# A spectral branch's first product as seven half-size products, beside an attention loop, on one Trainium2 core

## The chip, the core and the metric

The kernel runs on one core of one Trainium2 chip. The engines are named as in the profile: PE (TensorE, matrix products), DVE (VectorE), ACT (ScalarE), POOL (GpSimd) and SP (SyncE, which here issues every transfer); 16 DMA engines move data between device memory and the on-chip memory. The metric is the device time of one execution in microseconds.

## The reference

Two branches share nothing but the output, whose halves they fill. Branch A is attention with 32 heads of 32 and one key and value head (S = 2048, D = 1024); branch B is a two-dimensional Fourier mixing, written as matrix products.

```python
q = (x @ wq).reshape(B, S, H, Dh).transpose(0, 2, 1, 3)
k, v = x @ wk, x @ wv
p = softmax(einsum("bhqd,bkd->bhqk", q, k) * Dh ** -0.5)
a_out = einsum("bhqk,bkd->bhqd", p, v).transpose(0, 2, 1, 3).reshape(B, S, H * Dh) @ wo
...
a = einsum("bsd,ed->bse", xB, dft_hid_re)      # first product, real part
b = einsum("bsd,ed->bse", xB, dft_hid_im)      # first product, imaginary part
y = einsum("ts,bse->bte", dft_seq_re, a) - einsum("ts,bse->bte", dft_seq_im, b)   # second product
out = concatenate([a_out, y], axis=-1)
```

## The kernel before, in words

**Two kinds of work.** The attention loop runs over 32 units (a block of 512 queries and a group of four heads) of 32 steps each. A step `n` makes the scores of 128 queries against 1024 keys (`scores`, two matmuls into `pss`), takes the negated row maximum of them on DVE (`nm`), sums the exponentials of rows on ACT (`row_sums`, in place in `pss`, which has two buffers), and makes transposed scores of an earlier unit (`expo`, two matmuls into `pst`, which has one buffer, then an exponential on ACT into `p`). Every eighth step ends with `pv`, 16 products of probabilities with values, which DVE adds into `ov`.

Everything else is *filler*: the key, value and query projections, both products of branch B and the output projection. It is a list of groups (`add`, line 226). A group of 24 matmuls fills one 128 x 512 tile `psb` in PSUM: eight chunks of 128 rows, each with three matmuls, because each float32 factor is split in a high and a low part (`rh`, `rl` for the right factor of 128 x 512; `mh`, `ml` for the left one, of which one item covers four chunks). `take(n)` issues the next n filler matmuls; after a group's last one its `post` empties the tile.

**What sets the order.** Instructions of an engine run in program order (`Ordered`, line 42), and the order is written out by the loop at line 685. `level` (line 681) spreads the filler evenly: what is left after the prologue is divided over the 1024 steps, seven shares in each eight steps, none at the step with `pv`. `aside` (line 316) lets a group run on when a bank is wanted near its start or its end. Two PSUM banks (`ps_b`) serve the filler, `pv` and a small transpose in turn (`bank`, line 268).

**How factors come.** Two lines of items, `RL` for right and `ML` for left factors (lines 220 and 221), each with four steps: load from device memory, add a second source on GpSimd where there is one (`comb`; `nothing` for `RL`), cast to the high part (`hi`), subtract to get the low part (`lo`). Each step is issued a fixed number of filler matmuls ahead of the item's due time: 40, 40, 14 and 8 for `RL`, 52, 36, 27 and 21 for `ML`. Casts are on ACT before the loop and on DVE in it (line 153), subtractions on DVE. An item with `save` has both parts stored, and a later item with `pre` fetches them ready made. `load_y` (line 212) brings a tile that a group's `post` adds to, up to four at a time (`NY`).

**The stage that is changed.** `stage1` (line 383) makes the first product. Its four column blocks (r, e), real or imaginary part and half of the columns, each take 16 row blocks of one group of 24. `post` evicts the tile on ACT with the sign of r, stores it, and on GpSimd adds it to, or subtracts it from, an earlier block: these sums (`NAMES`, line 378) are the right factors of the second product. `stage2` (line 435) makes that product in seven products of half size in each direction (the table `PRODUCTS`, line 31: left terms, right terms, outputs with signs), each in two halves of the summed dimension that are joined in `h`; its left factors are added on GpSimd. Positions in the filler: key, value and query projections 0 to 864, `stage1` 864 to 2400, `stage2` to 5088, output projection to 5664, the last block's to 5856. The prologue ends at position 494.

Of the kernel before, what the change touches and what calls it, by code (L numbers as in the profile page):

```python
# [29 lines left out]

PRODUCTS = [
# [21 lines left out]
class Item:  # L53


    def __init__(self, srcs, save=None, pre=None):
        self.srcs, self.save, self.pre = srcs, save, pre
        self.need = self.last = self.due = self.t = None


class Group:


    def __init__(self, left, right, post, rows=P, ys=()):
        self.left, self.right, self.post, self.rows, self.ys = left, right, post, rows, ys


@with_exitstack
def tile_kernel(ctx: ExitStack, tc, xT, wq, wkv, wo, xbT, wT, cT, out):
# [19 lines left out]
    xb_d = [[[dram.tile([P, 4, P], F32, name=f"xb_{s}_{q}_{a}") for a in range(2)] for q in range(2)] for s in range(NC)]  # L89
# [14 lines left out]
    NR0, NM0, NY = 3, 3, 4  # L104
# [112 lines left out]
    def nothing(it):  # L217
        pass

    RL = Line(NR0, NR, (40, 40, 14, 8), load_r, nothing, hi_r, lo)  # L220
# [5 lines left out]
    def add(gs):  # L226

        for g in gs:
            i0 = len(groups) * 24
# [3 lines left out]
            for c, it in enumerate(g.right):  # L233
                if it.need is None:
                    it.need = i0 + 3 * c
                    p0 = prev["set"]
                    it.due = min(it.need, p0 + (i0 - p0) * (c + 1) // 8)
# [12 lines left out]
    prev = {"set": -200, "this": 0}  # L250

# [13 lines left out]
    cur = {"at": 0, "bank": None}  # L265
# [20 lines left out]
    def product(g, ps, j):  # L286
# [3 lines left out]
        te.matmul(ps[:g.rows], a, r.lo if w == 1 else r.hi, start=j == 0, stop=j == 23)  # L290

    def take(n):
        for _ in range(n):
            i, j = divmod(pos["fill"], 24)
            if i >= len(groups):
                return
            g = groups[i]
# [8 lines left out]
            if j == 23:  # L306
# [20 lines left out]
    qp = pool(ctx, "qp", 1)  # L327
# [4 lines left out]
    def kv_post(b):  # L332
        cols = slice(b * W, (b + 1) * W)

        def post(ps):
            kv = qp.tile([2 * DH, W], F32, name="kv")
            act.activation(kv, ps[:2 * DH], AF.Copy)
            dve.tensor_copy(kst[0:DH, cols], kv[0:DH])
            kl = qp.tile([DH, W], F32R, name="kl")
# [38 lines left out]
    NAMES = {}  # L378
    for _, nt, _ in PRODUCTS:
        key = tuple(nt)  # L380
        NAMES[key] = [dram.tile([P, W], F32, name=f"r{len(NAMES)}_{s}") for s in range(NC)]

    def stage1():
        seen = []
        for r, e in ((0, 0), (1, 1), (0, 1), (1, 0)):
            ws = [Item([(lambda c=c, r=r, e=e: wT[r, e, c], 1)]) for c in range(ND)]
            sg = -1 if r else 1
            todo = [k for k in NAMES if len(k) == 2 and all(t[:2] in seen + [(r, e)] for t in k)
                    and any(t[:2] == (r, e) for t in k)]
            seen.append((r, e))  # L390
# [376 lines left out]
```

## Time and profile before

| | |
|---|---|
| median of three runs (lowest to highest) | 2896.22 us (2896.21 to 2896.61) |
| the profiled execution: its time, its span | 2893.22 us, 2891.4 us |
| granted TensorE clock, mean of the span | 0.999 |
| ACT busy, share of the span | 2279.2 us, 79% |
| DVE busy, share of the span | 1995.0 us, 69% |
| transfers in the span | 485.03 MB, mean 168 GB/s |
| transfers issued in `stage1` by line of the page | loads 32 + 32, saves 64, fetches 192, results 64, sums 80 read and 80 written |

The page gives, in this order: busy time of each engine, the span in 40 slices, the DMA queues, the chain of work that ended last, the costliest groups of instructions, and the transfers. A row of the groups reads: source line, engine, operation, the tile that is written `<-` the tiles that are read, shapes, `x` the number of instructions, then busy time in us and the mean of one in ns, then the idle time of the engine just before them and what ended it. All engine instructions pass through the helper at line 50, so rows are told apart by their tiles, and a group's window in time by the counts of its rows. A row of the timeline has the start, the duration, the instruction and in brackets the idle time before it. A row of the waits has the waiting engine and tile, the releaser, the total in us, how often, and the longest. Matmuls overlap in PE's pipeline, so that their pitch, the distance between starts, is shorter than the duration shown. SPq is SP's queue.

### The profile page before, as it was taken

The numbers are of one execution on the slowest core, as the hardware profiler recorded it, in microseconds if no ns is written. First come the engines' busy times: TensorE is split into PE (matmuls) and PEld (weight loads), VectorE is DVE, ScalarE is ACT, GpSimd is POOL, SyncE is SP. The second block draws the span as 40 slices with busy tenths as digits, with TensorE's granted clock in tenths as the row PEclk, the third lists the DMA queues.
The fourth block names the chain that finished last, engine by engine and source line by source line (L and its number), as shares of the span: only waits on it lengthen the run. The fifth ranks groups of instructions, "written<-read, shape, count | busy, mean of one in ns | idle before, by whom it ended". The sixth has DMA issues, their size and how long they took to land.

```text
span 2891.4 us, 39967 instructions
## 1 busy us (share of the span) xinstructions
PE 2839.5 (98%) x14096; PEld 1957.6 (68%) x14096; DVE 1995.0 (69%) x2593; ACT 2279.2 (79%) x3342; POOL 467.8 (16%) x342
## 2 busy tenths in 40 slices
PE   7999999999999999999999999999999999999999
PEld 5876667666666766666666666766666666666666
DVE  6866677555565656888788887778887787765510
ACT  4688888888888888888887887878878788888851
POOL 0000000011121223222223230022232220120000
PEclk9999999999999999999999999999999999999999
DMA  8865455555666667455355453264454432454455
GB/s 301 284 197 168 168 183 184 166 169 186 200 206 218 226 221 238 122 153 164 107 173 160 131 176 114 86 191 140 138 149 139 146 122 84 142 168 130 134 155 169
DMA packets 318025, 485.03 MB, mean 168 GB/s; under 512 B 33664, under 2 KB 98688, under 8 KB 317824
## 3 DMA queue, kind: packets, MB, share of 16 engines
q1 hardware_dynamic: 317824, 482.48, 53.3%
q8 instruction: 111, 1.82, 0.3%
q14 instruction: 90, 0.74, 0.1%
HBM read 351.54 MB, written 129.76 MB: 166 GB/s over the span
## 4 chain that ended last, share of the span: by engine, by line
PE 45%; issue 6%; DVE 4%; ACT 3%; DMA 3%; POOL 2%; SPq 0%; POOLq 0%; ACTq 0%
PE psb L50 29%; PE pst L50 9%; PE pss L50 8%; DVE nm L50 2%; DMA y<-y 1%; ACT p L50 1%; POOL y L50 1%; ACT pss L50 1%; DVE mh L50 1%; DMA m<-in_cT_dram 1%; SPq L50 0%; DVE ml L50 0%; DMA y<-r 0%; DVE rl L50 0%; POOL m L50 0%
## 5 line engine op out<-in xcount | busy, mean ns | idle before, releaser
L50 DVE TENSOR_REDUCE nm<-pss 128x1 f32<-128x1024 f32 x1024 | 1250.6, 1222 | 361.9 <-PE pss L50 358.8
L50 ACT ACTIVATE p<-pst 128x1024 f32<-128x1024 f32 x1024 | 1054.0, 1029 | 395.8 <-PE pst L50 389.3
L50 ACT ACTIVATE pss<-pss,nm 128x1024 f32<-128x1024 f32 x1024 | 1117.5, 1091 | 104.5 <-DVE nm L50 95.2
L50 PE MATMUL psb<-rh,mh 128*128 128x512 f32 (+1 forms) x1916 | 754.9, 394 | 10.3 <-ACT rh L50 8.0
L50 PE MATMUL psb<-rh,ml 128*128 128x512 f32 (+1 forms) x1916 | 754.4, 394 | 0.5 <-DVE ml L50 0.5
L50 PE MATMUL psb<-rl,mh 128*128 128x512 f32 (+1 forms) x1916 | 754.0, 394 | 0.3 <-DVE rl L50 0.3
L50 PE MATMUL pst<-qst,kst 128*128 128x512 f32 x2048 | 660.8, 403 | 17.3 <-ACT p L50 16.7
L50 PE MATMUL pss<-kst,qst 128*128 128x512 f32 x2048 | 657.5, 402 | 12.4 <-ACT pss L50 11.7
L50 PEld LDWEIGHTS pss<-kst,qst 128*128 128x128 f32 x2048 | 372.7, 188 | 202.6 <-issue 86.4
L50 PEld LDWEIGHTS pst<-qst,kst 128*128 128x128 f32 x2048 | 367.3, 188 | 155.3 <-ACT p L50 77.9
L50 PE MATMUL psb<-p,v 128*32 128x512 f32 x4096 | 466.0, 595 | 0.0
L50 PEld LDWEIGHTS psb<-rh,mh 128*128 128x128 f32 (+1 forms) x1916 | 358.8, 187 | 97.5 <-ACT rh L50 9.0
L50 PEld LDWEIGHTS psb<-rl,mh 128*128 128x128 f32 (+1 forms) x1916 | 358.8, 187 | 87.0 <-DVE rl L50 1.4
L50 PEld LDWEIGHTS psb<-rh,ml 128*128 128x128 f32 (+1 forms) x1916 | 358.7, 187 | 86.8 <-DVE ml L50 1.4
L50 PEld LDWEIGHTS psb<-p,v 128*32 128x32 f32 x4096 | 120.0, 109 | 276.0 <-issue 269.1
L50 POOL TENSOR_TENSOR m<-m,m 128x512 f32<-128x512 f32 x160 | 215.3, 1352 | 462.5 <-DMA m<-in_cT_dram 398.4
L50 DVE TENSOR_TENSOR ov<-ov,psb 128x512 f32<-128x512 f32 x96 | 66.0, 688 | 292.9 <-PE psb L50 292.9
L50 ACT ACTIVATION_READ_ACCUMULATOR pss<-pss,nm 128x1 f32 x1024 | 213.5, 209 | 0.0
L50 DVE TENSOR_TENSOR ml<-m,mh 128x512 fp32r<-128x512 f32 (+1 forms) x274 | 198.1, 723 | 4.0 <-ACT mh L50 3.6
L50 POOL TENSOR_TENSOR y<-y,h 128x512 f32<-128x512 f32 x64 | 91.7, 1443 | 564.8 <-DVE h L50 505.9
L50 DVE CAST mh<-m 128x512 fp32r<-128x512 f32 x267 | 145.2, 544 | 21.6 <-POOL m L50 15.1
L50 POOL MEMSET qst<- 32x2048 f32 x32 | 58.5, 1833 | 564.7 <-PE pst L50 454.6
(63 smaller groups left out, 798.2 us busy)
## 6 DMA issues: line engine op xcount, KB each, us to landing
m<-in_cT_dram SPq DMA_DIRECT2D x384, 256.0 KB, 3.7
r<-r SPq DMA_DIRECT2D x112, 256.0 KB, 3.7
mh<-xb SPq DMA_DIRECT2D x96, 256.0 KB, 3.9
ml<-xb SPq DMA_DIRECT2D x96, 256.0 KB, 4.1
y<-y SPq DMA_DIRECT2D x96, 256.0 KB, 2.9
y<-r SPq DMA_DIRECT2D x80, 256.0 KB, 3.1
r<-y SPq DMA_DIRECT2D x80, 256.0 KB, 2.0
qst<-qh SPq DMA_DIRECT2D x64, 256.0 KB, 5.7
```

The costliest lines, as they stand in the source:

```text
L50: return lambda *a, **k: self.tc.keep_in_program_order(f(*a, **k))
```

## The change

The first product is made for two pairs of column blocks, `((0, 0), (1, 1))` and then `((1, 0), (0, 1))`. For each pair, seven products of half the size in rows, in the summed dimension and in columns take the place of eight (table `STAGE1`: name, left terms, right terms, and for each output the partial sum that it adds to, the sign, and where it goes). A product has eight groups, one for each row block of a half, and a group has four chunks, so 12 matmuls. The tables' counts over the seven products are 12 left terms, 12 right terms and 8 outputs, of which 7 add to a partial sum.

Partial sums (`t`, `u2`, `u3`, `u4`) are stored in device memory and loaded again; DVE adds the PSUM tile to the loaded one, only the first product's tile is evicted on ACT. Left and right factors with two or three terms are added on GpSimd in `comb`, now for `RL` too; the third source of a left item and the second and third of a right one lie in tiles `h`, which `stage2` uses later. The combined left and right factors of `p6` are also stored as they are (`raw`), because `p3` and `p4` use them. The first pair saves its split left factors, the second fetches them. `NY` becomes 6. The real and imaginary blocks keep their sign, so `PRODUCTS` has other signs and another order, and `stage2` needs no copies with a changed sign. A group's length is now its own (`g.n`), which also enters `add`, `take` and `aside`. The tiles of the key and value eviction come from the pool `yp`, and their own pool is gone.

```diff
 PRODUCTS = [
-    ([(1, 1, 1)], [(1, 0, 1), (0, 0, -1)], [(0, 0, 1), (1, 0, 1)]),
...
-    ([(1, 0, 1), (1, 1, -1)], [(1, 0, 1), (1, 1, 1)], [(0, 0, 1)]),
+    ([(0, 0, 1), (1, 1, 1)], ((0, 0), (1, 1)), [(0, 0, 1), (1, 1, 1)]),
+    ([(0, 1, 1), (1, 1, 1)], ((0, 0),), [(1, 0, 1), (1, 1, -1)]),
...
+    ([(1, 1, 1)], ((1, 0), (0, 0)), [(0, 0, -1), (1, 0, -1)]),
+]
+SUB = ((0, 0), (1, 1))
...
+STAGE1 = [
+    ("p1", [(0, 0, 1)], [(0, 0, 1)], [(None, 1, "t")]),
+    ("p2", [(0, 1, 1)], [(0, 1, 1)], [("t", 1, (0, 0))]),
+    ("p6", [(1, 0, 1), (1, 1, 1), (0, 0, -1)], [(1, 1, 1), (1, 0, -1), (0, 0, 1)], [("t", 1, "u2")]),
+    ("p7", [(0, 0, 1), (1, 0, -1)], [(1, 1, 1), (1, 0, -1)], [("u2", 1, "u3")]),
+    ("p5", [(1, 0, 1), (1, 1, 1)], [(1, 0, 1), (0, 0, -1)], [("u2", 1, "u4"), ("u3", 1, (1, 1))]),
+    ("p3", [(0, 1, 1), ("p6", -1)], [(1, 1, 1)], [("u4", 1, (0, 1))]),
+    ("p4", [(1, 1, 1)], [("p6", 1), (0, 1, -1)], [("u3", -1, (1, 0))]),
 ]
...
-    xb_d = [[[dram.tile([P, 4, P], F32, name=f"xb_{s}_{q}_{a}") for a in range(2)] for q in range(2)] for s in range(NC)]
+    xb_d = [[[dram.tile([P, 4, P], F32, name=f"xb_{f}_{k}_{a}") for a in range(2)] for k in range(8)] for f in range(7)]
+    xr_d = [dram.tile([P, 4, P], F32, name=f"xr_{k}") for k in range(8)]
+    wr_d = [[dram.tile([P, W], F32, name=f"wr_{n}_{c}") for c in range(4)] for n in range(2)]
+    u_d = {(n, k): [dram.tile([P, W], F32, name=f"{k}_{n}_{s}") for s in range(8)] for n in range(2) for k in ("t", "u2", "u3", "u4")}
...
-    NR0, NM0, NY = 3, 3, 4
+    NR0, NM0, NY = 3, 3, 6
...
             return
-        it.t = [r0p.tile([P, W], F32, name="r0")]
-        sp.dma_start(it.t[0], it.srcs[0][0]())
+        it.t = []
+        for n, (ap, _) in enumerate(it.srcs):
+            if n == 0:
+                it.t.append(r0p.tile([P, W], F32, name="r0"))
+            else:
+                it.t.append(spare(0, 5))
+            sp.dma_start(it.t[-1], ap())
 
...
-            t = m0p.tile([P, 4, P], F32, name=f"m{n}", bufs=NM0 - n)
+            if n < 2:
+                t = m0p.tile([P, 4, P], F32, name=f"m{n}", bufs=NM0 - n)
+            else:
+                t = spare(5, 3).rearrange("p (a b) -> p a b", a=4)
             it.t.append(t[:, :a.shape[1], :a.shape[2]])
...
+    turn = {0: 0, 5: 0}
+
+    def spare(first, n):
+
+        turn[first] += 1
+        return hp.tile([P, W], F32, name=f"h{first + turn[first] % n}")
+
     def comb(it):
-        if not it.pre and len(it.t) > 1:
-            (gp.tensor_add if it.srcs[1][1] > 0 else gp.tensor_sub)(it.t[0], it.t[0], it.t[1])
+        if it.pre:
+            return
+        for t, (_, sg) in zip(it.t[1:], it.srcs[1:]):
+            (gp.tensor_add if sg > 0 else gp.tensor_sub)(it.t[0], it.t[0], t)
+        if it.raw is not None:
+            sp.dma_start(it.raw, it.t[0])
...
-    RL = Line(NR0, NR, (40, 40, 14, 8), load_r, nothing, hi_r, lo)
+    RL = Line(NR0, NR, (40, 40, 14, 8), load_r, comb, hi_r, lo)
...
-            i0 = len(groups) * 24
+            i0 = g.at = end[0]
+            end[0] += g.n
...
-                it.due = i0 + 24
+                it.due = i0 + g.n
...
+            if j == g.n - 1:
+                cur["group"] += 1
...
-        j = pos["fill"] % 24
-        if pos["fill"] >= len(groups) * 24 or j == 0:
+        if cur["group"] >= len(groups):
             return
-        if j < 6:
+        g = groups[cur["group"]]
+        j = pos["fill"] - g.at
+        if 0 < j < 6:
             take(6 - j)
-        elif j > 17:
-            take(24 - j)
-
...
+    NAMES = {nt: [dram.tile([P, W], F32, name=f"r{i}_{s}") for s in range(NC)] for i, (_, nt, _) in enumerate(PRODUCTS)}
+    singles = {k[0]: t for k, t in NAMES.items() if len(k) == 1}
...
     def stage1():
+        done = []
+        for n, cols in enumerate((((0, 0), (1, 1)), ((1, 0), (0, 1)))):
+            for f, (name, lt, rt, outs) in enumerate(STAGE1):
+                keeps = any(t[0] == name for p in STAGE1 for t in p[1] + p[2])
+
+                def x_src(t, k):
+                    if isinstance(t[0], str):
+                        return (lambda: xr_d[k], t[1])
+                    return (lambda: xbT[t[0] * 8 + k, :, t[1] * 4:t[1] * 4 + 4], t[2])
+
+                def w_src(t, c):
+                    if isinstance(t[0], str):
+                        return (lambda w=wr_d[n][c]: w, t[1])
+                    r, e = cols[t[0]]
+                    return (lambda: wT[r, e, t[1] * 4 + c], t[2])
+
+                R = [Item([w_src(t, c) for t in rt], raw=wr_d[n][c] if keeps else None) for c in range(4)]
+                for k in range(8):
+                    if n:
+                        left = [Item(None, pre=lambda f=f, k=k: xb_d[f][k])]
+                    else:
+                        left = [Item([x_src(t, k) for t in lt], save=xb_d[f][k], raw=xr_d[k] if keeps else None)]
+                    ys, plan = [], []
+                    for frm, sg, to in outs:
+                        it = None
+                        if frm is not None:
+                            it = Item([(lambda frm=frm, n=n, k=k: u_d[n, frm][k], 1)])
+                            ys.append(it)
+                        more = []
+                        if not isinstance(to, str):
+                            me = cols[to[1]]
+                            s = to[0] * 8 + k
+                            for key in NAMES:
+                                if len(key) == 2 and me in key:
+                                    o = key[0] if key[1] == me else key[1]
+                                    if (o, s) in done:
+                                        yo = Item([(lambda o=o, s=s: right_of((o,), s), 1)])
+                                        ys.append(yo)
+                                        more.append((key, yo))
+                            done.append((me, s))
+                        plan.append((it, sg, to, more))
+
+                    def post(ps, plan=plan, n=n, k=k, cols=cols):
+                        for it, sg, to, more in plan:
+                            if it is None:
+                                o = op.tile([P, W], F32, name="qh")
+                                act.activation(o, ps, AF.Copy)
+                            else:
+                                o = it.y
+                                (dve.tensor_add if sg > 0 else dve.tensor_sub)(o, o, ps)
+                            if isinstance(to, str):
+                                sp.dma_start(u_d[n, to][k], o)
+                                continue
+                            me, s = cols[to[1]], to[0] * 8 + k
+                            if me in singles:
+                                sp.dma_start(singles[me][s], o)
+                                ready.add(((me,), s))
+                            for key, yo in more:
+                                if key != SUB:
+                                    gp.tensor_add(yo.y, yo.y, o)
+                                elif me == key[0]:
+                                    gp.tensor_sub(yo.y, o, yo.y)
+                                else:
+                                    gp.tensor_sub(yo.y, yo.y, o)
+                                sp.dma_start(NAMES[key][s], yo.y)
+                                ready.add((key, s))
+                    yield Group(left, R, post, ys=ys)
...
-        for mt, nt, outs in PRODUCTS[1:] + PRODUCTS[:1]:
+        for mt, nt, outs in PRODUCTS:
...
```

More of the change, by code (lines that the diff above doesn't have):

```diff
@@ L65, in __init__ @@
         self.left, self.right, self.post, self.rows, self.ys = left, right, post, rows, ys
+        self.n = 3 * len(right)
 @with_exitstack
@@ L250, in tile_kernel @@
     prev = {"set": -200, "this": 0}
+    end = [0]
     def pump():
@@ L263, in run_later @@
             later.pop(0)[1]()
-    cur = {"at": 0, "bank": None}
+    cur = {"at": 0, "bank": None, "group": 0}
     used = [0, 0]
@@ L316, in aside @@
     def aside():
-        j = pos["fill"] % 24
-        if pos["fill"] >= len(groups) * 24 or j == 0:
+        if cur["group"] >= len(groups):
             return
-        if j < 6:
+        g = groups[cur["group"]]
+        j = pos["fill"] - g.at
+        if 0 < j < 6:
             take(6 - j)
-        elif j > 17:
-            take(24 - j)
-    qp = pool(ctx, "qp", 1)
+        elif j > g.n - 6:
+            take(g.n - j)
     def x_set(b):
@@ L676, in tile_kernel @@
     PRO = pos["fill"]
-    FILL = len(groups) * 24
+    FILL = end[0]
     LAST = 24
@@ L701, in tile_kernel @@
     last = groups[len(groups) - 8:]
-    take((len(groups) - 8) * 24 - pos["fill"] - 12)
+    take(last[0].at - pos["fill"] - 12)
     pv(len(units) - 1, 3)
@@ L706, in tile_kernel @@
     hi7, lo7 = lse["out"]
-    take((len(groups) - 8) * 24 - pos["fill"])
+    take(last[0].at - pos["fill"])
     def first_part(g, ps):
```

62 lines of the change are left out of this document (6 added, 56 removed), and 9 rows, old and new, of the table PRODUCTS.

## The prediction

> **What bounds the kernel now.** I read the page's engine shares first, then a table of busy time by stage, then the groups and waits of the stages.
>
> ```profile
> span 2891.4 us, 39967 instructions
> ...
> PE 2839.5 (98%) x14096; PEld 1957.6 (68%) x14096; DVE 1995.0 (69%) x2593; ACT 2279.2 (79%) x3342; POOL 467.8 (16%) x342
> ```
>
> PE is busy for 98% of the span, with no other engine near it. One product matmul and the pitch at which PE takes them stand in PE's timeline:
>
> ```profile
> 711.54 0.40 PE L50 MATMUL psb<-rh,ml 128*128 128x512 f32 x1
> ...
> 713.85 0.40 PE L50 MATMUL psb<-rh,ml 128*128 128x512 f32 x1
> ...
> 721.80 3.64 PE L50 MATMUL psb<-p,v 128*32 128x512 f32 x32
> ```
>
> Between the first two starts lie ten matmuls (six of the products, two of pss, two of pst), so one costs 2.31 / 10 = 0.231 us of PE time; the 0.40 is its pipelined length. The 16 probability-value products of every eighth step (32 records) hold PE for about 3.6 us.
>
> The stage that is changed lies from 353 to 1148 us. The groups in that window show it: 3 x 513 product matmuls (its own 64 x 24 = 1536, with an edge) and 610 / 2 = 305 attention steps. What follows up to 2568 us is the second product, which has the kind of preparation that the change brings into the first.
>
> ```profile
> L50 PE MATMUL psb<-rh,ml 128*128 128x512 f32 x513 | 201.5, 393 | 0.0
> ...
> L50 PE MATMUL pst<-qst,kst 128*128 128x512 f32 x610 | 195.1, 401 | 3.8 <-ACT p L50 3.7
> ...
> L50 PE MATMUL psb<-p,v 128*32 128x512 f32 x1216 | 138.3, 595 | 0.0
> ...
> L50 ACT ACTIVATE qh<-psb 128x512 f32<-128x512 f32 (+1 forms) x64 | 38.2, 596 | 5.1 <-PE psb L50 4.7
> ...
> L50 DVE TENSOR_TENSOR rl<-r,rh 128x512 fp32r<-128x512 f32 x32 | 22.8, 714 | 0.1
> L50 DVE TENSOR_TENSOR ml<-m,mh 128x512 fp32r<-128x512 f32 x32 | 21.8, 680 | 0.0
> ...
> L50 DVE CAST rh<-r 128x512 fp32r<-128x512 f32 x32 | 17.2, 539 | 0.2 <-PE psb L50 0.2
> ...
> L50 DVE CAST mh<-m 128x512 fp32r<-128x512 f32 x32 | 14.4, 450 | 0.0
> ```
>
> By stage (columns PE, PEld, DVE, ACT, POOL, granted clock, DMA share, GB/s):
>
> ```profile
> 353.00:1148.00 795.00, 789.82 (x3985) 546.46 (x3984) 491.05 (x590) 668.95 (x990) 119.86 (x90) 1.00 0.61 199
> 1148.00:2568.00 1420.00, 1397.79 (x6989) 953.71 (x6988) 1136.43 (x1520) 1159.00 (x1687) 333.93 (x238) 1.00 0.46 141
> ```
>
> The clock is granted in full throughout. Pure PE work is (1536 + 1220) x 0.231 + 38 x 3.6 = 773 us in the first stage, whose 795 us are 2.8% more; and (2688 + 2140) x 0.231 + 67 x 3.6 = 1357 us in the second, whose 1420 are 4.7% more. The DVE share goes from 491 / 795 = 62% to 1136 / 1420 = 80% between them. That is the relation I rest on: PE sets the pace, and the busier DVE is, the more of it is lost in short waits. PE's waits in the second stage pass through ACT, which waits for the row maxima from DVE:
>
> ```profile
> PE pst L50 <- ACT p L50: 12.3, 44, 0.7
> PE pss L50 <- ACT pss L50: 7.5, 13, 1.9
> ```
>
> **The change part by part.** *PE.* Removed: 64 groups of 24 = 1536 matmuls; added: 2 x 7 x 8 groups of 12 = 1344. The matmuls have the same shape, so 192 x 0.231 = 44.4 us go. They go from the whole loop, not from the stage alone: line 683 spreads what is left after the prologue (position 494) over 1024 steps, so a step takes (5472 - 494 - 24) / 1024 = 4.84 fillers in place of 5.03. PE remains the slowest engine with them, so I count all 44.4. Each half of the new stage (one pair of column blocks) has 672 fillers, thus 139 steps, and 672 x 0.231 + 556 x 0.231 + 17.4 x 3.6 = 346 us of pure PE work; with the 2.8% of today's stage, 356 us.
>
> *ACT.* 64 evictions of 0.596 become 16, and 8 sign copies in the second product go: 34 us less on an engine that is 84% busy here. No price; it makes room.
>
> *DVE.* The rows of the second stage give the prices with GpSimd at work beside it:
>
> ```profile
> L50 DVE TENSOR_TENSOR ml<-m,mh 128x512 fp32r<-128x512 f32 x222 | 163.3, 735 | 0.0
> L50 DVE CAST mh<-m 128x512 fp32r<-128x512 f32 x222 | 125.3, 564 | 15.3 <-POOL m L50 15.1
> ...
> L50 DVE TENSOR_TENSOR rl<-r,rh 128x512 fp32r<-128x512 f32 x112 | 85.0, 759 | 0.5
> ...
> L50 DVE CAST rh<-r 128x512 fp32r<-128x512 f32 x112 | 57.7, 515 | 1.7 <-PE psb L50 1.7
> L50 DVE TENSOR_TENSOR h<-h,psb 128x512 f32<-128x512 f32 x55 | 37.3, 678 | 1.6 <-PE psb L50 1.4
> ```
>
> Today's stage spends 491 - 32 x (0.450 + 0.680) - 32 x (0.539 + 0.714) = 415 us on attention, 1.36 a step. The first half of the new stage has 139 x 1.36 = 189, plus 56 left factors x 1.30 = 73, 28 right factors x 1.27 = 36 and 56 adds of a partial sum x 0.678 = 38: 336 of 356 us, 94% (some 90% as busy time, since neighbours overlap a little in the groups' sums). The second half fetches its left factors ready made: 263 of 356, 74%. Lost PE time was 2.8% at 62% and 4.7% at 80%. At 92%, between the two figures, a straight line gives 6.0%; a law that rises as share / (1 - share) gives 10.7%. For the first half this is 11 to 27 us more than today's 2.8%; I take 15, near the line, since the rows support only the line. For the second half 4.0% by the line: 4 us.
>
> What such a wait looks like, and that Pool has a part in it, is seen at 2150 us, in the timelines of DVE, POOL and PE:
>
> ```profile
> 2150.87 1.52 DVE L50 CAST rh<-r 128x512 fp32r<-128x512 f32 x1
> ```
> ```profile
> 2149.54 2.57 POOL L50 TENSOR_TENSOR m<-m,m 128x512 f32<-128x512 f32 x2
> ```
> ```profile
> 2156.20 0.73 PE L50 MATMUL pss<-kst,qst 128*128 128x512 f32 x2 [1.92 <-ACT pss L50]
> ```
>
> The cast takes 1.52 us rather than 0.5 and ends as Pool's pair of adds does (2152.1); four more casts and subtractions stand in DVE's queue between the row maxima; PE then stands for 1.92 us.
>
> *Pool.* In the first half 40 additions for left factors, 20 for right ones and 16 for sums of column blocks; in the second 20 and 64. At 1.352 us that is 103 and 114 us of 356, so Pool itself isn't short:
>
> ```profile
> L50 POOL TENSOR_TENSOR m<-m,m 128x512 f32<-128x512 f32 x157 | 211.4, 1353 | 460.7 <-DMA m<-in_cT_dram 396.7 <-DVE ml L50 21.7 <-DVE rl L50 18.3
> ```
>
> Its part in DVE's prices: between the stages a left factor's cast and subtraction went from 1.130 to 1.299 us, 222 x 0.169 = 37 us over 236 Pool instructions, 0.16 us each, and is contained in the sums above. [...] What full blocking would do is a rival below.
>
> *PSUM banks.* The stage's own wait for such a bank, and the reduction that stands in DVE's queue:
>
> ```profile
> PE psb L50 <- DVE ov L50: 0.6, 2, 0.5
> ```
> ```profile
> L50 DVE TENSOR_REDUCE nm<-pss 128x1 f32<-128x1024 f32 x1024 | 1250.6, 1222 | 361.9 <-PE pss L50 358.8
> ```
>
> A group's bank is now emptied by a DVE add, twice for the fifth product, behind whatever DVE has queued. Five in twelve of the 35 value products in the stage find a group that ended six matmuls before, some 2.3 us; an add behind one row maximum is 1.22 + 0.69. From 0 (today 0.6 us in the whole stage) to 35 x 5 / 12 x 0.7 = 10 us; I take 2, near the row.
>
> *Transfers and SP.* All are of 256 KB:
>
> ```profile
> m<-in_xbT_dram SPq DMA_DIRECT2D x32, 256.0 KB, 3.5
> ...
> y<-r SPq DMA_DIRECT2D x80, 256.0 KB, 3.1
> ```
>
> Today's stage issues 64 loads of factors, 64 saves, 192 fetches, 64 results, 80 reads and 80 writes of sums: 544. The first half now issues 96 + 48 loads, 112 saves, 12 raw sums, 56 reads and 32 writes of partial sums, 32 results, 16 reads and 16 writes: 420, or 110 MB. The second has 112 fetches, 48, 4, 56, 32, 64, 64: 380, or 100 MB. Attention adds 199 - 544 x 0.262 MB / 795 us = 20 GB/s. In 356 us these are 329 and 300 GB/s where today has 199. How much the engines can carry:
>
> ```profile
> 10.00:15.00 5.00, 5.00 (x21) 2.85 (x20) 4.97 (x8) 4.68 (x8) 0.00 (x0) 1.00 1.06 396
> ...
> 60.00:65.00 5.00, 5.00 (x18) 4.05 (x17) 3.06 (x6) 0.60 (x1) 0.00 (x0) 0.74 1.05 405
> ...
> 1030.00:1040.00 10.00, 10.00 (x61) 5.82 (x60) 4.43 (x5) 7.25 (x11) 2.80 (x3) 1.00 1.03 255
> 1130.00:1140.00 10.00, 10.00 (x63) 6.17 (x61) 8.63 (x16) 8.03 (x14) 3.99 (x4) 1.00 0.94 311
> ```
>
> With a deep queue of loads 396 to 405; in this stage, loads and stores mixed, once 255 at a full share and once 311 at 0.94. The third product alone (80 issues in 51 us) asks for over 400, and lives on the first two, which ask for 36 and 44. A left factor is loaded 52 matmuls ahead and added 36 ahead, 8 us for a landing of 3.5. SP's issues cost 0.32 to 0.42:
>
> ```profile
> 723.95 0.32 SPq L50 DMA_DIRECT2D r<-y  x1
> 724.32 0.42 SPq L50 DMA_DIRECT2D y<-r  x1
> ```
>
> The third product's ten per group are 4 of its 6.4 us, and a raw sum's store makes SP wait for Pool, with the next loads behind it. From 0 to a stage at the pace of its transfers (a rival); I take 3 us, because PE's waits hold only this one for a transfer in all of today's span:
>
> ```profile
> PE pss L50 <- DMA m<-in_cT_dram: 0.5, 1, 0.5
> ```
>
> *Sum.* -44.4 + 15 + 4 + 2 + 3 = -20 us. The profiled execution took 2893.2 (its span and 1.8 around it), so 2873; the median of the runs is 3.0 above it, so **2876 us**.
>
> **The rivals.** *Nothing is given back:* the factors are ready 21 matmuls (11 us) ahead, and DVE's lateness stays below that. For it: in the second stage 80% of DVE cost PE only 22 us of recorded idle time. 2896 - 44 = 2852 us. Against it: row maxima have no such lead, only two score buffers.
>
> *SP and Pool fall behind:* each runs its list in order; right factors are loaded and added at the same lead, so Pool stands for a landing with a left factor's add behind it, and DVE's cast behind that. A wait of 1 us at each of the 32 such additions' groups more than forecast, less what DVE's other losses hide: some 10 to 20 us, 2888. For it: 15.1 us of DVE's casts already wait for Pool's m. Against it: leads of 9 matmuls between the add and the cast.
>
> *Transfers set the pace (slower):* the stage has 210 + 14 = 224 MB. It decides when the rate falls under 224 MB / (712 + 44.4 + 5.8 us) = 294 GB/s; at 280, between the mixed rows, it lasts 799 us, 87 more: 2896 - 44 + 87 = 2939. For it: the row of 255. Against it: 396 and more in deep queue, and a share below 1 wherever less is asked. [...]
>
> *Pool blocks DVE outright (slower):* with 1.352 us lost per Pool instruction, the first half has 189 + 56 x 1.130 + 28 x 1.253 + 38 + 103 = 428 us of DVE, the second 263 + 114 = 377: 93 over, 2896 - 44 + 93 = 2945. [...]
>
> That the matmuls aren't saved can't be: the loops fix their number.
>
> **How the numbers follow.** Forecast 0.53, nothing given back 0.16, SP and Pool 0.17, transfers 0.11, blocking 0.03. A measurement of this kernel tells about 0.2%, 5.8 us, from no change. The forecast's unknowns reach from 2867 (11 and 4, nothing for banks and transfers) to 2896 (27, 4, 10 and 3). The range goes from the first rival to just over the third case: 2851 to 2897; below and above it lie 0.05 and 0.13. Faster: 0.53 + 0.16 + two thirds of 0.17 = 0.80; same: the rest of that and a mild form of the transfers, 0.08; slower 0.12.
>
> **What would show it.** Right: 13904 PE records; the stage at some 735 us; DVE near 90% in its first half and 75% in the second; PE's waits in the first half through ACT and nm, as at 2156 us; casts near 0.56. Wrong: waits of Pool or DVE for x, w or partial sums, DMA share at 1 with landings far over 4 us (transfers); casts over 1 us on average (blocking); PE idle of under 1% in the first half (nothing given back).

## The result, and the profile after

The changed kernel takes 3010.36 us (median of 4 runs, 3008.70 to 3011.86) against 2896.41 for the kernel before (4 runs, 2896.21 to 2896.94): a ratio of 1.0391, 95% interval 1.0376 to 1.0407, so 114 us slower where 20 us faster were forecast. The profiled execution took 3009.57.

The page of the changed kernel, engine shares and the granted clock in 40 slices:

```profile
span 3007.8 us, 40294 instructions
...
PE 2847.9 (95%) x13904; PEld 1927.5 (64%) x13904; DVE 2134.1 (71%) x2801; ACT 2248.2 (75%) x3286; POOL 581.7 (19%) x422
...
PEclk9999998999999999999999999999999999999999
```

There are 192 matmuls fewer, as planned, but PE's busy time is 8 us higher, not 44 lower, and its share fell to 95%. By stage: the first half of the new first product, its second half, and the second product (columns as in the prediction, from PE to GB/s).

```profile
353.00:761.00 408.00, 369.71 (x1779) 243.39 (x1778) 312.50 (x427) 295.93 (x431) 108.27 (x79) 0.96 0.83 284
761.00:1212.00 451.00, 384.85 (x1813) 251.89 (x1812) 271.62 (x337) 296.10 (x430) 120.91 (x90) 0.94 0.73 240
1212.00:2673.00 1461.00, 1430.93 (x7134) 970.28 (x7133) 1176.75 (x1556) 1191.97 (x1739) 338.51 (x239) 1.00 0.44 138
```

The halves last 408 and 451 us where 356 without new waits were worked out. Two things are seen in each row: PE stands for 38 and 66 us, and its clock is granted only at 0.96 and 0.94. PE's waits inside the stage:

```profile
PE psb L66 <- DVE y L66: 33.6, 13, 10.2
PE pss L66 <- ACT pss L66: 27.8, 14, 8.2
PE psb L66 <- DMA mh<-xb: 24.8, 9, 8.5
PE pst L66 <- ACT p L66: 8.1, 29, 0.7
```

They are few and long, up to 10 us; before, the whole stage had 4.3 us of them. The longest, in views of SP's queue, POOL, DVE and PE at the same moment. SP's queue:

```profile
442.10 0.48 SPq L66 DMA_DIRECT2D r<-in_wT_dram  x1
442.70 1.60 SPq L66 DMA_DIRECT2D h<-in_wT_dram  x2
450.77 0.33 SPq L66 DMA_DIRECT2D wr<-r  x1
451.14 0.92 SPq L66 DMA_DIRECT2D m<-in_xbT_dram  x2
```

POOL:

```profile
448.15 2.60 POOL L66 TENSOR_TENSOR r<-r,h 128x512 f32<-128x512 f32 x2 [13.75 <-DMA h<-in_wT_dram]
450.71 1.26 POOL L66 TENSOR_TENSOR m<-m,m 128x512 f32<-128x512 f32 x1
452.05 1.26 POOL L66 TENSOR_TENSOR m<-m,h 128x512 f32<-128x512 f32 x1
```

DVE, and PE:

```profile
442.10 1.22 DVE L66 TENSOR_REDUCE nm<-pss 128x1 f32<-128x1024 f32 x1
453.34 2.11 DVE L66 CAST mh<-m 128x512 fp32r<-128x512 f32 x1 [10.02 <-POOL m L66]
```
```profile
457.23 6.10 PE L66 MATMUL psb<-p,v 128*32 128x512 f32 x32 [10.20 <-DVE y L66]
```

To be read from the top: SP asks for the three terms of a right factor between 442.1 and 444.3, and Pool's list has their addition next, because load and addition are issued at the same position. Pool stands until 448.15 for the landing and adds until 450.7. A left factor's addition, whose own sources had been asked for from 437.3 on, stands behind it and ends at 453.3. DVE has reached that factor's cast and waits 10 us; the row maxima behind it, and the add that empties PSUM for the value products, come later; PE stops for 10.2 us. Meanwhile SP stands in front of `wr<-r`, the store of the sum, from 444.3 to 450.8, and asks for nothing else.

What follows the gap is slow too: the 32 records of the value products take 6.10 us, where the prediction's row from the kernel before has 3.64. From 450 to 460 the clock is granted at 0.50 (last three columns: clock, DMA share, GB/s):

```profile
440.00:450.00 10.00, 6.83 (x28) 4.74 (x27) 3.32 (x5) 4.61 (x7) 1.77 (x2) 0.93 0.71 268
450.00:460.00 10.00, 2.77 (x16) 0.79 (x20) 5.96 (x5) 2.73 (x4) 7.90 (x6) 0.50 0.82 271
460.00:470.00 10.00, 10.00 (x50) 5.77 (x41) 6.38 (x9) 6.11 (x10) 0.00 (x0) 0.89 1.04 338
```

A part of that low clock passes while PE stands, so its price is read from PE's busy time: 370 + 385 = 755 us here, and 364 + 366 = 729 us in the third run below, for the same matmuls (3592 and 3593 records). That leaves, as an estimate, some 25 us for the clock. PE stands for 104 us here and for 29 us there. The low clock isn't seen beside long gaps alone: 22 us later, after waits of 0.67 and 1.93 us, pairs of matmuls take 1.22 us in place of 0.63, and the clock is granted at 0.50.

```profile
474.02 0.63 PE L66 MATMUL pss<-kst,qst 128*128 128x512 f32 x2
...
476.93 0.50 PE L66 MATMUL psb<-rh,mh 128*128 128x512 f32 x1 [0.67 <-DVE y L66]
479.36 1.22 PE L66 MATMUL pss<-kst,qst 128*128 128x512 f32 x2 [1.93 <-ACT pss L66]
```
```profile
479.40:482.60 3.20, 3.20 (x7) 2.28 (x8) 3.20 (x6) 2.99 (x5) 0.00 (x0) 0.50 0.91 267
```

Counted from PE's timeline, the seven products of the two halves last as follows (96 fillers each; an even pace would be 51 us, give or take 4 for the value products that fall into one). The last three columns belong to the experiments below, with the first and the second half in each.

| product | prepared meanwhile | changed, first half | second half | loads earlier | nine buffers | both |
|---|---|---|---|---|---|---|
| p1 | right factors of one term | 50 | 55 | 50, 55 | 50, 55 | 50, 55 |
| p2 | of three terms | 68 | 68 | 59, 55 | 69, 67 | 56, 50 |
| p6 | of two | 69 | 62 | 56, 58 | 70, 54 | 54, 54 |
| p7 | of two | 57 | 48 | 57, 48 | 62, 48 | 55, 48 |
| p5 | of one | 50 | 68 | 50, 68 | 50, 65 | 49, 63 |
| p3 | of two | 65 | 71 | 61, 68 | 64, 65 | 63, 56 |
| p4 | of one | 48 | 80 | 48, 72 | 48, 67 | 48, 57 |

In the first half, time is lost only where right factors of two or three terms are prepared. In the second half it is also lost in p5, p3 and p4, where a group reads back three or four tiles.

### The profile page after: what moved, and what is told of

Read it like the earlier page. It is cut to its first block, busy times and chain, and to the rows that moved or that the text cites. A ratio compares the mean times of both kernels' runs of the same rounds, so it can differ in the third digit from the quotient of the medians.

```text
span 3007.8 us, 40294 instructions
## 1 busy us (share of the span) xinstructions
PE 2847.9 (95%) x13904; PEld 1927.5 (64%) x13904; DVE 2134.1 (71%) x2801; ACT 2248.2 (75%) x3286; POOL 581.7 (19%) x422
## 3 DMA queue, kind: packets, MB, share of 16 engines
q8 instruction: 109, 1.79, 0.2%
## 4 chain that ended last, share of the span: by engine, by line
PE 54%; DVE 7%; DMA 6%; ACT 3%; issue 3%; POOL 2%; SPq 1%; POOLq 0%; ACTq 0%; DVEq 0%
PE psb L66 35%; PE pst L66 10%; PE pss L66 9%; DVE nm L66 3%; ACT p L66 2%; DMA r<-y 2%; ACT pss L66 1%; POOL y L66 1%; DMA m<-in_cT_dram 1%; DVE rl L66 1%; DVE ml L66 1%; SPq L66 1%; DVE mh L66 1%; DVE ov L66 1%; DMA ml<-xb 1%
## 5 line engine op out<-in xcount | busy, mean ns | idle before, releaser
L66 PE MATMUL psb<-rh,mh 128*128 128x512 f32 (+1 forms) x1852 | 734.5, 397 | 38.3 <-DMA mh<-xb 24.8
L66 PE MATMUL psb<-rh,ml 128*128 128x512 f32 (+1 forms) x1852 | 733.2, 396 | 0.5 <-DMA ml<-xb 0.4
L66 PE MATMUL psb<-rl,mh 128*128 128x512 f32 (+1 forms) x1852 | 732.7, 396 | 0.3 <-DVE rl L66 0.3
L66 PE MATMUL psb<-p,v 128*32 128x512 f32 x4096 | 478.9, 609 | 29.5 <-DVE y L66 29.5
L66 PEld LDWEIGHTS psb<-rh,mh 128*128 128x128 f32 (+1 forms) x1852 | 349.0, 188 | 128.3 <-issue 19.0
L66 PEld LDWEIGHTS psb<-rh,ml 128*128 128x128 f32 (+1 forms) x1852 | 349.0, 188 | 86.0 <-DMA ml<-xb 1.7
L66 POOL TENSOR_TENSOR m<-m,m 128x512 f32<-128x512 f32 x192 | 263.4, 1377 | 532.9 <-DMA m<-in_cT_dram 387.5
L66 DVE TENSOR_TENSOR ml<-m,mh 128x512 fp32r<-128x512 f32 (+1 forms) x298 | 224.9, 755 | 3.9 <-ACT mh L66 3.6
L66 DVE CAST mh<-m 128x512 fp32r<-128x512 f32 x291 | 157.7, 542 | 62.6 <-POOL m L66 54.8
L66 DVE TENSOR_TENSOR rl<-r,rh 128x512 fp32r<-128x512 f32 x220 | 173.3, 788 | 3.9 <-ACT rh L66 3.1
```

The lines of the kernel that those rows point to most:

```text
L66: return lambda *a, **k: self.tc.keep_in_program_order(f(*a, **k))
```

## The experiments

Runs 1 to 4 are single executions beside a single one of the kernel before (2891.95); runs 6 and 7 are single ones beside a median of twelve (2894.40). Single executions of one of these kernels lie up to 9 us apart (run 12), so smaller differences between them say little.

**1. Right factors loaded earlier.**

```diff
-    RL = Line(NR0, NR, (40, 40, 14, 8), load_r, comb, hi_r, lo)
+    RL = Line(NR0, NR, (56, 40, 14, 8), load_r, comb, hi_r, lo)
```

> Right factors are loaded 56 filler matmuls ahead in place of 40, their addition on GpSimd stays at 40. Changed kernel: 3010 us; its stage lasts 859 us, 147 above the 712 that the forecast had without new waits. By products (96 fillers, 51 us without waits) the first half loses 17, 18, 7 and 14 us in exactly the four products during which right factors of two or three terms are prepared, and nothing in the other three; the second half loses 17, 11 and 20 in three of the same places and 17 and 29 in two others. Theory A (GpSimd's list stands for the landing of a right factor that was asked for at the same position, with left factors' additions and SP's stores behind it): the first half gets back most of its 55 us, the second some 20 to 40 of its 95, so 2920 to 2945 us. Rival B (too few buffers for partial sums, SP stands in front of their loads): under 15 us, and only in the second half. Rival C (the transfers' rate is the limit, 329 GB/s in the first half): the same bytes, no change, 3000 to 3015 us.

Measured: 2952.3 us, 58 less. The direction and the places are A's (p2 and p6 in the first half fell from 68 and 69 to 59 and 56), the size is less than A's: by the table each half gives back some 27 us, where A had most of 55 for the first. DVE's wait for left factors in the stage, in the changed kernel and in this run:

```profile
DVE mh L66 <- POOL m L66: 43.8, 14, 10.0
```
```profile
DVE y L66 <- DMA y<-u: 39.3, 16, 6.4
...
DVE mh L66 <- POOL m L66: 8.5, 3, 3.8
```

The wait for left factors is nearly gone. The wait for partial sums that land too late has grown, from 29.2 us in the changed kernel to 39.3.

**2. Nine buffers in the second half.**

```diff
     def load_y(it):
-        it.y = yp.tile([P, W], F32, name="y0")
+        if it.third:
+            it.y = hp.tile([P, W], F32, name=f"h{5 + it.third % 3}")
+        else:
+            it.y = yp.tile([P, W], F32, name="y0")
...
-        while ydone[0] < min(len(ylist), yused[0] + NY) and ylist[ydone[0]].due - 24 <= pos["fill"]:
+        while ydone[0] < min(len(ylist), yused[0] + room_y()) and ylist[ydone[0]].due - 24 <= pos["fill"]:
```

> In the second half, partial sums and column blocks that are read back use nine buffers in place of six (three tiles that are free there), and may be asked for nine ahead; nothing else changes. Theory A: the second half gets 0 to 15 us back, the first half nothing, 2995 to 3010. Rival B: the second half's fifth and seventh product (three and four reads per group) lose their 17 and 29 us and part of the others' 48, 2940 to 2970. Rival C: no change, or slower, since more is in flight at once.

Measured: 2989.67 us, 21 less, and only in the second half (p6, p3, p4, a little p5). It lies between A's and B's figures. With six buffers, SP's list in the second half of the changed kernel stands for stores to leave a buffer:

```profile
SPq L66 <- DMA r<-y: 39.0, 33, 4.2
SPq L66 <- DMA u<-y: 18.0, 9, 3.2
```

A load that needs the buffer waits there, and all that is behind it. With nine buffers both rows are gone from SP's longest; no wait for a transfer has over 6.7 us there.

**3. Both.**

> Both edits of the two runs before. A alone: as the first, 2920 to 2945. B alone: as the second. If A holds in the first half and B in the second: the savings add, 2880 to 2915. C: 3000 to 3015.

Measured: 2908.53 us, 102 less. The two savings are 58 and 21 alone and 102 together: each wait hid a part of the other. The halves are now 376 and 382 us, and the clock is nearly back:

```profile
354.00:730.00 376.00, 363.54 (x1778) 240.62 (x1777) 320.04 (x427) 295.49 (x431) 111.56 (x79) 1.00 0.91 309
730.00:1112.00 382.00, 365.87 (x1815) 245.61 (x1814) 266.63 (x337) 295.35 (x430) 123.11 (x90) 0.99 0.85 284
```

The same bytes pass at 309 and 284 GB/s that passed at 284 and 240. C, the rate as the limit of the changed kernel, falls here.

**4. Both, and ready-made factors fetched earlier** (36 ahead in place of 27).

```diff
                     it.need = it.due = i0 + 12 * c
+                    if it.pre and g.n == 12:
+                        it.due -= 9
```

> As the third, and the second half's ready-made left factors are fetched 36 matmuls ahead in place of 27 (PE stood 25 us for them in the changed kernel). If those waits follow from SP standing in front of other loads (A, B), they are gone in the third run already and this one is within 8 us of it; if the fetch itself is asked for too late, it is 10 to 25 us under the third. C: no change.

Measured: 2915.63 us, 7 more than the third run, so nothing is gained, as A and B have it. PE's waits for the fetched factors (`mh<-xb`) had gone from 24.8 us in the changed kernel to 5.2 in the third run without an earlier fetch: most of the fetches were late because SP stood elsewhere.

**5. Left factors kept for both column pairs.** The two pairs take turns within a product; a left factor is made once and used twice.

```diff
+        order = [(0, 0)] + [x for k in range(1, 8) for x in ((k, 0), (k - 1, 1))] + [(7, 1)]
...
-                        left = [Item([x_src(t, k) for t in lt], save=xb_d[f][k], raw=xr_d[k] if keeps else None)]
+            lefts = [[Item([x_src(t, k) for t in lt], raw=xr_d[k] if keeps else None)] for k in range(8)]
```

> For each of the seven products the two column pairs take turns (row block k of the first, row block k-1 of the second), so a left factor is added and split once and used twice without being stored: 112 stores and 112 fetches go, 16 stores of column blocks that are now needed later come; the eight right factors of a product are prepared over 192 fillers. Right factors are loaded 56 ahead, and nine buffers serve the partial sums of the last three products. 592 transfers in place of 800: some 240 GB/s over the stage; DVE's work on left factors is spread over the whole stage, some 84% throughout in place of 90 and 75. Theory C' (what the third run still loses, 46 us over 712, is the transfers' rate and the DVE's peak in the first half): the stage lasts 725 to 745 us, 2872 to 2890 us in all, below the kernel before. Rival (what is left is the order of the lists, which stays much as it was): 2895 to 2915.

Measured: 2897.58 us (2894.09 to 2900.53) against 2894.4; ratio 1.0011 (1.0001 to 1.0021). The stage lasts 748 us, 10 less than in the third run and just over the span given. In its two halves, and in the second product:

```profile
353.00:730.00 377.00, 366.49 (x1828) 245.21 (x1828) 285.62 (x369) 303.01 (x446) 89.07 (x65) 1.00 0.58 188
730.00:1105.00 375.00, 361.56 (x1781) 241.78 (x1781) 310.51 (x394) 292.20 (x422) 147.17 (x105) 1.00 0.81 269
1105.00:2560.00 1455.00, 1425.36 (x7110) 966.37 (x7109) 1171.52 (x1548) 1185.44 (x1731) 336.52 (x239) 1.00 0.46 137
```

The two windows of the stage move 188 and 269 GB/s in 752 us where 309 and 284 took 758. C' fails for the transfers: with a quarter of the bytes gone (172 MB for 225) little is gained. For DVE's peak it isn't tested, since the peak moved more than it spread: DVE is busy for 286 and 311 us of the halves, where the third run has 320 and 267. The time lies in the rival's span, but not for the rival's reason, since PE's waits for loads and sums in the stage fell from 9.4 to 0.5 us. Nearly all that PE's waits still show there is for ACT:

```profile
PE pss L66 <- ACT pss L66: 12.7, 18, 1.2
PE pst L66 <- ACT p L66: 9.7, 38, 0.7
```

**6. Additions later instead of loads earlier** (40 and 24 in place of 40 and 40).

> The changed kernel, with the right factors' loads where they were (40 ahead) and only their addition on GpSimd moved back to 24. Theory A (what counts is the distance between load and addition): about as the run with earlier loads, 2940 to 2965 us. Rival (the right factors come too late for their use, so that an earlier load is what helped): 3000 to 3020, or worse, since the addition is now later. Rival C (rate): 3000 to 3015.

Measured: 2943.14 us, 67 less than the changed kernel. It is the distance between load and addition that counts: A holds, and the rival of factors too late for their use is out.

**7. More bytes.** A second store of each high part, to a place that nothing reads, on top of the third run.

```diff
+            if it.again is not None:
+                move(sp, it.again, it.hi)
```

> The third run (both edits, 2908.5 us) with 56 extra stores of 256 KB in the first half, each a second copy of a high part to a place that nothing reads: 14.7 MB more on 117, 12.5%, and 56 x 0.4 = 22 us more of SP's issue time in some 376 us. If the rate binds in the first half there (309 GB/s at a DMA share of 0.91): the half is 30 to 47 us longer, 2938 to 2955. If only the order of the lists binds: within 12 us, 2905 to 2920.

Measured: 2917.86 us, 9 more than the third run. The first half goes from 376 to 379 us:

```profile
354.00:733.00 379.00, 363.19 (x1777) 240.51 (x1776) 315.37 (x427) 295.67 (x431) 110.44 (x79) 1.00 0.98 343
```

343 GB/s at a share of 0.98 for 379 us: the rate of the third run had 11% to spare.

**8. The first term by itself: 192 matmuls fewer in the kernel before.**

```diff
-            ws = [Item([(lambda c=c, r=r, e=e: wT[r, e, c], 1)]) for c in range(ND)]
+            ws = [Item([(lambda c=c, r=r, e=e: wT[r, e, c], 1)]) for c in range(ND - 1)]
```

(and the group length as in the change).

> The kernel before with 192 matmuls left out and nothing put in their place: each of the first product's 64 groups has 21 matmuls (the eighth chunk of the summed dimension is left out, with its four right factors), so branch B's result lacks that chunk. It prices the first term of the forecast by itself. If PE sets the pace everywhere and 0.231 us is what a matmul is worth (the forecast): 44 us under the kernel before, 2850. Rival (with fewer fillers between two attention steps, the waits through ACT and DVE in the second product and the output projection grow; after the first product the changed kernel and the run with kept factors are 18 us longer than their added steps explain): 24 to 30 us under it, 2865 to 2871.

Measured: 2875.34 us (2873.31 to 2880.33) against 2894.27; ratio 0.9940 (0.9925 to 0.9955). The 192 matmuls are worth 19 us (13 to 22), less even than the rival's figure. First and second product, before (795 and 1420 us) and here:

```profile
355.00:1071.00 716.00, 710.86 (x3592) 488.00 (x3591) 454.88 (x543) 608.64 (x908) 118.40 (x89) 1.00 0.67 219
1071.00:2538.00 1467.00, 1433.43 (x7135) 970.54 (x7134) 1173.31 (x1554) 1196.82 (x1749) 339.77 (x239) 1.00 0.45 137
```

The second product, untouched, lasts 47 us longer, because with fewer fillers a step its 2688 are spread over 555 steps in place of 535. By blocks of eight steps, from one value product to the next, that is 21.2 us before and 21.1 here, though each block has 1.5 matmuls less (0.34 us). In the first product a block goes from 20.8 to 20.5, about the whole price. Blocks scatter by about 1 us, so that a mean over the 67 blocks of the second product is good to some 0.1: there a filler seems to be worth less than its price, and how much less isn't settled by this run.

**9. Right factors' casts on ACT** (on the fifth kernel, with additions 24 ahead).

```diff
+            if it.slot is not None:
+                act.activation(it.hi, it.t[0], AF.Copy)
+            else:
+                cast(it.hi, it.t[0])
```

> The run with kept factors (2897.6), with the addition of right factors 24 ahead (56 loaded) and the stage's 56 casts of right factors on ACT in place of DVE: 28 us less on DVE, 35 more on ACT, which evicts 48 tiles less than the kernel before. If DVE's list is what the stage's remaining 36 us wait for: 2885 to 2893, below the kernel before (2894.4 on that chip). If ACT is as short as DVE (it is what PE waits for directly): 2896 to 2905.

Measured: 2907.99 us (2905.18 to 2914.15), ratio 1.0057 (1.0040 to 1.0074). Slower than the fifth, and a little beyond the figure for "ACT is as short as DVE". Since two things were changed, run 12 tries later additions alone, at other leads.

**10 and 11. Two rates of fillers,** on the fifth and on the eighth kernel.

```diff
-        take(int((FILL - PRO - LAST) * x) + PRO - pos["fill"])
+        if x < X1:
+            take(int((END1 - PRO) * x / X1) + PRO - pos["fill"])
+        else:
+            take(int((FILL - LAST - END1) * (x - X1) / (1 - X1)) + END1 - pos["fill"])
```

> The run with kept factors (2897.6), with the fillers spread at two rates: 1714 up to the end of the first product over the first 379 steps (4.52 a step), the rest at 5.03 a step, as the kernel before has it in the second product and the output projection. Theory D (there a block of eight steps lasts 21.1 us with 38.7 fillers as with 40.2, because the chain of row maxima on DVE and exponentials on ACT sets it, so fillers are free; in the first product they are paid): what follows the first product goes back from 1744 to some 1693 us, the first product lasts 16 steps longer but each step has less: 755 to 770 us for 748. 2860 to 2875 in all. Rival E (the uneven spread only moves the same waits about, every filler costs its 0.23 us): 2893 to 2900.

> The kernel before with the same 192 matmuls left out (branch B's first product lacks the last chunk of its sum) and the two rates of the run beside it, so that every block of eight steps up to the end of the first product has 36.2 fillers in place of 40.2 and the others what they had. Theory D: the blocks of the first product and the projections get the whole 47 x 4.06 x 0.231 = 44 us, 2848 to 2858 against 2875 with the even spread. Rival E: 2872 to 2878, as with the even spread. In between (2860 to 2870) if the attention chain begins to bind at 36.2.

Measured: the tenth 2900.03 us (ratio 1.0021, 1.0011 to 1.0030), the eleventh 2871.95 (2871.40 to 2873.09; ratio 0.9924, 0.9908 to 0.9941). Both totals lie at the edge of E's spans and far from D's. The second product goes back to 1430 us in the tenth and 1426 in the eleventh, over 536 steps. The tenth's blocks in the first product last 780 / 297 x 8 = 21.0 us with 36 fillers, and the eleventh shows

```profile
370.00:1121.00 751.00, 741.53 (x3728) 500.77 (x3727) 474.43 (x574) 642.68 (x966) 120.59 (x90) 1.00 0.64 209
1121.00:2547.00 1426.00, 1400.42 (x6992) 955.56 (x6991) 1143.49 (x1521) 1158.22 (x1687) 335.30 (x238) 1.00 0.46 140
```

Blocks of eight steps, by fillers in a block (whole blocks from one value product to the next, from PE's timeline):

| | PE's work alone | query projections | first product | second product |
|---|---|---|---|---|
| before, 40.2 | 20.3 | 20.9 | 20.8 | 21.2 |
| run 8, 38.7 | 19.9 | 20.5 | 20.5 | 21.1 |
| run 11, 36.2 (second product 40.1) | 19.4 | 20.2 | 20.2 | 21.3 |
| run 5, 38.7 | 19.9 | 20.5 | 21.5 | 21.0 |
| run 10, 36.2 (second product 40.1) | 19.4 | 20.2 | 21.0 | 21.3 |

From 40.2 to 36.2 PE's work falls by 0.9 us and the block by 0.6 to 0.7 in the stages with little preparation. In the second product some 1.4 fillers, 0.33 us of PE work, are worth 0.1 us between the kernel before and run 8, 0.2 between runs 8 and 11, and 0.3 between runs 5 and 10. D, fillers that cost nothing there, isn't borne out; nor is E's full price for every filler, since the 192 matmuls gave 19 us in run 8 and 23 in run 11.

**12. The fifth kernel with additions later** (48 and 28).

> The run with kept factors (2897.6), with right factors loaded 48 and added 28 fillers ahead (20 between the two, as against 16 at 56 and 40), casts on DVE as there. If Pool still stands for right factors there in a way that PE pays for (DVE waited 11 us for left factors behind them): 2888 to 2894. If what is left is the attention chain through DVE and ACT, on which the order of Pool's list has no bearing: 2895 to 2900.

Measured: 2903.82 us (2900.90 to 2910.19), ratio 1.0035 (1.0024 to 1.0047). That is above both spans, so later additions gain nothing here. That the attention chain is what is left, as the rival has it, isn't shown by this. Part of run 9's loss may be its later additions; how much the casts add stays open.

## Why the prediction was wrong

*Where the 114 us come from.* 192 matmuls: -19 (run 8). What the third run still loses against that: 2908.5 - (2892 - 19) = 36, or 33 with the later median of the kernel before (2894.4). The order of the lists and the buffers: 102. Together 116 to 119; the middle term is a remainder, so the sum is no check of its own.

*The bound.* "PE remains the slowest engine with them, so I count all 44.4" is the first step that failed. The count of matmuls and the 0.231 us were right; their worth was 19 us (run 8). A PE that is busy for 98% by pipelined lengths was taken as the only pace, and the 4.7% that the second product has over its PE work was taken as a loss that goes along with it. Yet run 8's blocks there became only 0.1 us shorter with 0.34 us less to do. Why 25 of the 44 us didn't come back stays open. PE's waits for `p` and `pss` there, 57 times with 19.8 us, which the forecast quoted, point at the attention chain through DVE and ACT, but no run changed that chain by itself, and runs 5 and 10 differ there by nearly the full price.

*The order of the lists.* The second step that failed, and by far the dearer one, is the price of the rival "SP and Pool fall behind": the sum has nothing for it, and the 3 us for transfers and SP are the nearest term. It had the mechanism: right factors loaded and added at the same lead, Pool standing for a landing, a left factor's addition behind it, DVE's cast behind that. It was given 1 us at each of 32 places, and a chance of 0.17. It cost up to 10 us at a place, because the wait passes through four lists in turn, and PE's clock was low besides (0.96 and 0.94 in the halves, 1.00 and 0.99 in the third run); moving the load or the addition by 16 matmuls alone gave 58 and 67 us back (runs 1 and 6). That the left factor's add has 9 matmuls, some 5 us, before its cast stood in the text; the sum of a landing of 4 us, two additions of 1.3 and two more for the left factor is 9 us, and could have been made from the rows there.

*Partial sums.* The six buffers were not weighed at all: the fifth product's groups in the second half read four tiles each, so that a buffer must be stored, freed and loaded again within one and a half groups. Cost: 21 us alone, 44 once the other wait is gone (2952.3 - 2908.5).

*What held.* DVE's share was forecast at some 90% and 75% of the halves; in the third run it is 320 / 376 = 85% and 267 / 382 = 70%. The terms for DVE, banks and transfers, 15 + 4 + 2 + 3 = 24 us, stand against the 33 to 36 that the third run loses. Banks as such cost little: PE's waits for `y` went from 33.6 to 2.7 us with the lists in order. The rival "transfers set the pace" fell with runs 3 and 7: at 343 GB/s the half was 3 us longer, so the 255 of one window was not a ceiling. "Pool blocks DVE outright" fell as a price for every Pool instruction: casts of left factors took 0.58 us on average in the changed kernel, not over 1. Single DVE instructions do take longer while Pool adds: 17 of 56 subtractions in the fifth run, 1.66 to 1.79 us for 0.67 to 0.71 (last section). "Nothing is given back" was far off.

The predicted signs of a right forecast were partly there (13904 records, casts of 0.58 us), but DVE's shares were 77% and 60% in the changed kernel's longer halves, and the stage's 859 us for 735 and waits behind landings, named as signs of a wrong one, were there as well.

## What to carry to other kernels

Before work is taken off the engine that looks busiest, leave out as much of it as the change would and time that: it costs one run, and here it showed 19 us for 44. In a kernel whose engines each work off a list in written order, a transfer and its first user should not be issued at the same position (16 matmuls more between them gave 58 and 67 us here); add up landing and work along all lists that a late operand passes through, and compare the sum with the lead of the next user in the list. Two such faults hide each other: each repair alone gave 58 and 21 us, both 102.

## What was not expected of the hardware

In the changed kernel PE's granted clock was 0.50 from 450 to 460, where a gap of 10.2 us ended, and 0.96 and 0.94 over the halves, while before it stood at 1.00 in both stages. From 479.4 to 482.6, after waits of 0.67 and 1.93 us, it was 0.50 again.

In the seventh run the 16 DMA engines carried 343 GB/s of mixed loads and stores for 379 us; the transfers that the changed kernel's page lists are of 256 KB each.

In the fifth run DVE's subtraction for right factors took 1.009 us on average, with Pool's additions beside it, against 0.714 in the first product of the kernel before and 0.805 in the changed one:

```profile
L66 DVE TENSOR_TENSOR rl<-r,rh 128x512 fp32r<-128x512 f32 x56 | 56.5, 1009 | 0.2
```

Its busy time there is 56 x 0.295 = 17 us above that of the kernel before. The mean hides two kinds (shortest, median and longest in ns):

```profile
L66 DVE TENSOR_TENSOR rl<-r,rh x56: 674/684/1787, 361.4 to 1099.7; 128x512 fp32r<-128x512 f32 x56
```

In the timelines 39 of the 56 take 0.67 to 0.71 us and 17 take 1.66 to 1.79. Each of the 17 began while an addition on Pool was under way; none of the 39 began with more than 0.2 us of one to go. One of the 17:

```profile
480.55 1.68 POOL L66 TENSOR_TENSOR y<-y,y 128x512 f32<-128x512 f32 x1 [4.50 <-DVE y L66]
```
```profile
480.99 1.79 DVE L66 TENSOR_TENSOR rl<-r,rh 128x512 fp32r<-128x512 f32 x1
```

Pool's addition ends at 482.23 and DVE's subtraction 0.55 us later. The 17 of 56, at some 1.1 us more each, make the 0.3 us of the mean.
